# Scores and products in halves between the quarters of the solo steps, eleven chunks paired, and ScalarE in source order for two more units

## The chip, the cores and the metric

The kernel runs on one core of a Trainium2 chip, as one program. The metric is its time on the device in microseconds. Beside it stands the span, from the first to the last instruction of one profiled execution. Engines are named as in the profile: PE (TensorE's matmuls) and PEld (its weight loads), DVE (VectorE), ACT (ScalarE), POOL (GpSimd) and SP (SyncE, which issues all DMAs here).

## The reference

Attention over chunks of 32 rows with a local context and 8 memory rows, and then, for each of four batches, a mixer: a low-rank product over the sequence (U, V) and a feed-forward layer of 512 to 2048 to 512. All in float32, and U, V and the weights come as float64.

```python
for c in range(nc):                       # 768 / 32 = 24 chunks, 8 heads, D = 64
    k_full = np.concatenate([mem_k, k[:, :, l_start:r_end]], axis=2)   # 16 left, 8 right
    v_full = np.concatenate([mem_v, v[:, :, l_start:r_end]], axis=2)
    scores = scale * np.matmul(q_c, k_full.transpose(0, 1, 3, 2))
    a = np.exp(scores - np.max(scores, axis=-1, keepdims=True))
    a = a / (np.sum(a, axis=-1, keepdims=True) + 1e-09)
    out[:, :, c_start:c_end] = np.matmul(a, v_full)
...
h = xt @ U @ V                            # rank 32, over the sequence
u = x + h.transpose(0, 2, 1)
return u + np.maximum(u @ w_ch1, 0.0) @ w_ch2
```

## The kernel before, in words

**The feed-forward part.** The 2048 hidden columns are cut into 16 chunks f of 128. A batch has 768 rows in two blocks of 384. For a block and a chunk, `w1_step` runs 12 matmuls into a bank of ps_h (L943): every factor is split into a high and a low part, and three of the four products are formed. ScalarE then writes relu's high part hh (L949), VectorE the low part hl (L950). `w2_step`, always of the unit before, runs 9 matmuls into three accumulators of 128 x 512 (L986 six, L991 three). One `w1_step` and the `w2_step` of its predecessor are called a unit here.

**Batch 0 is special** (`both_blocks`). The weights arrive as float64 and are decoded while it runs, so that for the first SPLIT = 12 chunks both blocks are computed in turn (units 0 to 23; block 0 one chunk ahead, LEAD = 1). The second block's three accumulators are the three banks of ps_a, which the attention otherwise uses. When they are given up (L957 adds them to x), the remaining four chunks run solo: block 0 in units 24 to 27, and then block 1 in units 28 to 31, in the order 15, 14, 12, 13. For chunks 12 and 13 block 1 fetches the low part of w1 (w1l) back from DRAM (`fetch_w1l`, L398). During the last eleven units the attention of batch 1 is computed: its generator is advanced by steps, of which PACE counts how many are taken by the end of each unit from BEGINL = 21 on. They are taken together: up to unit 24 behind `w2_step`, later between `w1_step` and `w2_step`. In later batches the same steps are spread evenly.

**Decoding.** `stream` takes a chunk through ScalarE (L185, the exponent words scaled: the begin), five operations of VectorE (L196, L200, L210, L215, L222), ScalarE's cast of the high part (`upper`, L333) and VectorE's subtraction for the low part (`lower`, L337). Chunks 0 and 1 go w1 and w2 by themselves, later ones both at once, six steps each. Its working buffers are tiles called dec while the front runs, and the two homes of v, vb, afterwards. A chunk's begin stands in the source in the middle of the decoding of the one before. Every unit takes RATE = 3 steps, every fourth one more.

**The attention** of a batch works in pairs T = 0, 1, 2 of 128-row tiles. `k_part` and `q_part` transpose half a pair's keys or queries on PE (L476), and ScalarE copies them out of PSUM (L499 to L507, L519). `s_turn` runs the scores of a pair, 128 matmuls of 64 x 32 by 64 (L535) into two banks; `s_weights` takes maximum, difference and exponential (L557, L558 on VectorE, L561 on ScalarE), `s_sums` the sums (L566). `t_part` transposes one bank of weights (L582, copied by L585). `av_part` runs the products with v, again 128 small matmuls into two banks (L597), which VectorE scales into x (L606). `load_v` brings v with ten or eleven DMAs a pair. At the end `collect` (L617, L623) forms U's part, `gs` and `g4` (L826 to L835) follow, and six matmuls L846 with L848 add V's part to x.

**Order.** PE runs in the source's order through batch 0 (`manual`, FRONT), SyncE in the whole kernel. VectorE and ScalarE follow the source during the head of batch 0 (HEAD, to L1083), that is, the whole attention of batch 0 up to "joined"; then VectorE in a manual schedule of its own (`paced`) until unit 24. All else is ordered by a scheduler that goes by its own estimate of times and may set instructions of a free engine ahead of earlier ones of the source. The head also runs V's and U's decoding, `spread_v` (L247, L252, L253), `turn_x` (L872) and the joins (L881 to L886, L896 to L918) that make the first two blocks' inputs. LOADS is the order of the head's DMAs on SyncE: t is q and k of a pair, v and w the v of a pair and the raw weights of a chunk.

PSUM has eight banks: three of ps_a, two of ps_h, three of ps_o (the accumulators of block 0).

```python
for n, (blk, f, where, begins, ends) in enumerate(units):
    ...
    hid_ = w1_step(0, blk, f, w1l)
    ...
    if n > 2 * SPLIT:
        next(first, None)
        for _ in range(pieces[n]):
            next(gen[0], None)
    if prev is not None:
        ...
        w2_step(0, *prev)
    if n <= 2 * SPLIT:
        for _ in range(pieces[n]):
            next(gen[0], None)
```

Of the kernel before, what the change touches and what calls it, by code (L numbers as in the profile page):

```python
# [22 lines left out]
HEAD = {ET.DVE, ET.Activation}  # L23
# [3 lines left out]
LOADS = 't0 mk t1 t2 uv mv v0 mm v1 v2 w0 w1 w2'  # L27
# [3 lines left out]
HIGH = 400  # L31
LEAD = 1
SPLIT = 12
# [4 lines left out]
BEGINL = 21  # L38
NLOAD = 1
NSOLO = 2  # L40
PACE = [1, 2, 3, 9, 13, 23, 27, 30, 34, 35, 36]
# [3 lines left out]
def chunk_attn_then_mixer_kernel(  # L45
# [355 lines left out]
    def attention(b, xs):  # L401
# [123 lines left out]
        def s_turn(T):  # L525

            qt = [qts.pop((T, h)) for h in range(2)]
            banks = [att_ps() for _ in range(2)]
            psv = [ps.rearrange("n (t k g w) -> n t k g w", t=2, k=2, g=2) for ps in banks]
            for t in range(2):  # L530
                for p in range(NPR):
                    for i in range(NI):
                        for s in range(2):
                            rows = slice(D * s, D * s + D)
                            nc.tensor.matmul(  # L535
                                out=psv[s][CK * i:CK * i + CK, t, p % 2, p // 2, :],
                                lhsT=qt[p // 2][rows, p % 2, NI * t + i, :],
                                rhs=kall[rows, NB * (T % 2) + NI * t + i, p, :], start=True, stop=True,
                            )
            return banks, psv  # L540
# [31 lines left out]

        def s_part(T):
            s_weights(T, *s_turn(T))
            s_sums(T)
# [11 lines left out]
        def av_part(T):  # L587

# [3 lines left out]
            for t in range(2):  # L592
                for j in range(4):
                    for i in range(NI):
                        for g in range(2):
# [5 lines left out]
                            )  # L601
            rs = rss.pop(T)
            for t in range(2):
# [7 lines left out]
                xs[(b, 2 * T + t)] = x  # L611

# [125 lines left out]
        else:  # L738
# [36 lines left out]
            if b == 1:  # L775
                load_both(2)
                yield
                s_part(0)
                yield
# [7 lines left out]
                yield from turns(2)  # L787
                yield from turn_p(0)
                s_part(1)
                yield  # L790
                av_part(0)
                yield
                yield from load_v(2)
                yield from turn_p(1)
                s_part(2)
                yield
                yield from turn_p(2)
                av_part(1)
                yield
# [14 lines left out]
            av_part(NP - 1)  # L814
            yield
# [119 lines left out]
    def w1_step(b, blk, f, w1l):  # L935
# [6 lines left out]
        for m, (w, u, c) in enumerate(parts):  # L942
            nc.tensor.matmul(  # L943
                out=ph[:, :TOK], lhsT=w[:, c, :], rhs=u[c], start=(m == 0), stop=(m + 1 == len(parts)),
            )
        hh = hid.tile([P, TOK], F32R, name="hh")
# [16 lines left out]
    def w2_step(b, blk, f, where, begins, ends, hh, hl):  # L963
# [19 lines left out]
        for tt in range(TB):  # L983
            sl = slice(tt * P, (tt + 1) * P)
            for m, (h, w) in enumerate(passes[:2]):
                nc.tensor.matmul(  # L986
                    out=acc[tt], lhsT=h[:, sl], rhs=w, start=(begins and m == 0), stop=False,
                )
        for tt in range(TB):
# [10 lines left out]
    def both_blocks(pieces, following):  # L1000
# [11 lines left out]
        prev = None  # L1012
        paced = ExitStack()
        paced.enter_context(tc.manual_schedule(engines={ET.DVE}))
        for n, (blk, f, where, begins, ends) in enumerate(units):
            while done[0] < min(2 * NF, 2 * f + 2):
                advance(1)
                more_w()
            if n == 2 * SPLIT:
# [9 lines left out]
            hid_ = w1_step(0, blk, f, w1l)  # L1029
# [6 lines left out]
            if n > 2 * SPLIT:  # L1036
                next(first, None)
                for _ in range(pieces[n]):
                    next(gen[0], None)
            if prev is not None:  # L1040
# [3 lines left out]
                w2_step(0, *prev)  # L1044
            if n <= 2 * SPLIT:
                for _ in range(pieces[n]):
                    next(gen[0], None)
            prev = (blk, f, where, begins, ends) + hid_
        following(lambda: w2_step(0, *prev))
# [22 lines left out]
    manual.enter_context(tc.manual_schedule(engines=FRONT))  # L1072
    head = ExitStack()
# [9 lines left out]
    head.close()  # L1083
# [4 lines left out]
    for b in range(B):  # L1088
# [3 lines left out]
        for n in range(2 * NF):  # L1092
            if b == 0:
                want = PACE[n - BEGINL] if n >= BEGINL else 0
            else:
                want = min(NPIECE, -(-NPIECE * (n + 1) // (2 * NF - 2)))
# [3 lines left out]
        def following_pair(last):  # L1100
            with tc.high_priority(offset=HIGH):
                for _ in range(TB):
                    next(gen[0])
            last()
# [9 lines left out]
        if b == 0:  # L1114
            both_blocks(pcs, following_pair)
# [37 lines left out]
```

## Time and profile before

| | us |
|---|---|
| median of 3 runs | 723.65 (723.29 to 727.45) |
| the profiled execution | 724.77 |
| its span, first to last instruction | 723.0 |
| PE busy in the span | 673.6 |
| VectorE busy | 310.5 |
| ScalarE busy | 187.8 |
| mean granted clock of TensorE | 0.969 |

The times in the lines below are counted from the span's start. In a timeline line stand the start, the time that it took (of several, from the first's start to the last's end), engine and line, the operation, output and inputs, the shapes, how many; and in brackets how long the engine was idle before it and what ended that wait. In the table of waits stand the total, how many, and the longest. "Issue" is time in which an engine waited for nothing that the profile shows. PEclk is the share of full speed at which TensorE's clock was granted. SPq is SyncE's queue of DMAs.

### The profile page before, as it was taken

The page shows a single profiled execution, that of the slowest core. Times are in us where ns is not written, and L with a number is a line of the kernel's source. Part 1 is how long each engine was busy: PE and PEld are TensorE (multiplying, and loading weights), DVE is VectorE, ACT ScalarE, POOL GpSimd, SP SyncE. Part 2 cuts the span into 40 slices and gives each one's busy share as a digit, 9 for nine tenths or more (in the row PEclk, how much of TensorE's full clock was granted, in tenths as well). Part 3 has the DMA queues.
Part 4 walks back from the last instruction along what each step waited for, and adds up shares of the span by engine and source line. Part 5 has one row for each costly group of instructions (what it writes and reads, how often), then busy time and mean ns, then how long its engine had stood idle before and what let it go on. Part 6 is the DMA issues. An engine that isn't in the chain of part 4 may idle for free.

```text
span 723.0 us, 14688 instructions
## 1 busy us (share of the span) xinstructions
PE 673.6 (93%) x6280; PEld 586.6 (81%) x6284; DVE 310.5 (43%) x584; ACT 187.8 (26%) x470; POOL 22.0 (3%) x47
## 2 busy tenths in 40 slices
PE   7756999998786999999999998999999999999997
PEld 5534889987675789998888997898888999899896
DVE  6838889999644352225322230144342321112112
ACT  4423343343531122322211123133121211111110
POOL 2000000013200000000000000000000000000000
PEclk9868999999998899999999998999999999999999
DMA  8693445532642087312411076422411132214211
GB/s 233 134 344 101 138 146 168 191 94 87 160 119 82 1 232 176 117 44 85 116 48 56 30 210 157 131 70 74 125 46 45 44 102 73 61 42 131 63 55 44
DMA packets 103512, 79.07 MB, mean 109 GB/s; under 512 B 49464, under 2 KB 83384, under 8 KB 103448
## 3 DMA queue, kind: packets, MB, share of 16 engines
q1 hardware_dynamic: 103448, 78.14, 37.4%
q8 instruction: 49, 0.80, 0.5%
q14 instruction: 15, 0.12, 0.1%
HBM read 66.45 MB, written 10.49 MB: 106 GB/s over the span
## 4 chain that ended last, share of the span: by engine, by line
PE 82%; SPq 7%; DVE 5%; DMA 3%; issue 2%; ACT 1%; POOL 0%; ACTq 0%; DVEq 0%
PE ps_h L943 36%; PE acc L986 21%; PE acc L991 10%; SPq L458 3%; PE ps_a L597 2%; PE ps_a L476 2%; PE ps_a L535 2%; PE ps_a L986 2%; SPq L440 1%; PE ps_a L582 1%; PE ps_a L991 1%; DMA rw<-in_moe_w_ch_dram 1%; PE ps_a L928 1%; DVE x L957 1%; DMA w1l<-w1ld 1%
## 5 line engine op out<-in xcount | busy, mean ns | idle before, releaser
L950 DVE SCALAR_TENSOR_TENSOR hl<-ps_h,hh 128x384 fp32r<-128x384 f32 x127 | 70.5, 555 | 294.8 <-ACT hh L949 294.7
L943 PE MATMUL ps_h<-uh,w1h 128*128 128x384 f32 x508 | 171.5, 339 | 4.5 <-ACT w1h L333 3.7
L943 PE MATMUL ps_h<-ul,w1h 128*128 128x384 f32 x508 | 173.1, 342 | 0.1
L949 ACT ACTIVATE hh<-ps_h 128x384 fp32r<-128x384 f32 x127 | 62.6, 493 | 402.1 <-PE ps_h L943 402.1
L986 PE MATMUL acc<-w,hh 128*128 128x512 f32 x600 | 162.9, 405 | 0.0
L986 PEld LDWEIGHTS acc<-w,hh 128*128 128x128 f32 x600 | 110.8, 191 | 22.8 <-issue 3.4
L943 PE MATMUL ps_h<-uh,w1l 128*128 128x384 f32 x508 | 111.5, 339 | 3.1 <-DMA w1l<-w1ld 2.6
L943 PEld LDWEIGHTS ps_h<-uh,w1h 128*128 128x128 f32 x508 | 95.7, 189 | 10.4 <-ACT w1h L333 4.0
L943 PEld LDWEIGHTS ps_h<-ul,w1h 128*128 128x128 f32 x508 | 95.8, 189 | 5.7 <-DVE ul L931 0.4
L943 PEld LDWEIGHTS ps_h<-uh,w1l 128*128 128x128 f32 x508 | 90.7, 190 | 4.2 <-DMA w1l<-w1ld 2.9
L991 PE MATMUL acc<-w,hl 128*128 128x512 f32 x300 | 86.1, 392 | 0.0
L991 PEld LDWEIGHTS acc<-w,hl 128*128 128x128 f32 x300 | 56.5, 188 | 12.9
L848 DVE TENSOR_TENSOR x<-ps_a,x 128x512 f32<-128x512 f32 x24 | 16.1, 688 | 38.7 <-PE ps_a L846 38.7
L535 PE MATMUL ps_a<-kall,qt 64*32 64x64 f32 x1344 | 22.0, 225 | 3.6 <-issue 2.8
L986 PE MATMUL acc<-w2last,hh 128*128 128x512 f32 x90 | 25.1, 416 | 0.0
L535 PEld LDWEIGHTS ps_a<-kall,qt 64*32 64x32 f32 x1344 | 18.0, 105 | 7.8 <-issue 6.1
L597 PE MATMUL ps_a<-vb,pT 64*32 64x64 f32 x1152 | 15.5, 236 | 9.2 <-issue 6.1
L561 ACT ACTIVATE pt<-pt 128x512 f32<-128x512 f32 x24 | 15.0, 634 | 31.2 <-DVE pt L558 31.2
L597 PEld LDWEIGHTS ps_a<-vb,pT 64*32 64x32 f32 x1152 | 13.5, 110 | 11.6 <-issue 10.2
L606 DVE TENSOR_TENSOR x<-ps_a,rs 128x256 f32<-128x256 f32 x44 | 15.7, 413 | 13.6 <-PE ps_a L597 12.0
L986 PEld LDWEIGHTS acc<-w2last,hh 128*128 128x128 f32 x90 | 17.1, 197 | 4.2 <-issue 1.0
L499 ACT COPY kall<-ps_a 128x256 f32<-128x256 f32 x40 | 17.3, 441 | 10.5 <-PE ps_a L476 10.5
(188 smaller groups left out, 646.1 us busy)
## 6 DMA issues: line engine op xcount, KB each, us to landing
w1l<-w1ld SPq DMA_DIRECT2D x98, 256.0 KB
rw<-in_moe_w_ch_dram SPq DMA_DIRECT2D x14, 512.0 KB
qraw<-in_q_dram SPq DMA_DIRECT2D x24, 256.0 KB
out_dram<-x SPq DMA_DIRECT2D x24, 256.0 KB
vb<-in_v_dram SPq DMA_DIRECT2D x56, 98.0 KB
raw<-in_moe_w_ch_dram SPq DMA_DIRECT2D x20, 256.0 KB
kraw<-in_k_dram SPq DMA_DIRECT2D x16, 256.0 KB
rw<-in_moe_w_ch_dram SPq DMA_DIRECT2D x16, 256.0 KB
```

What stands on the lines that cost most here:

```text
L458: nc.sync.dma_start(out=vt[r0:r0 + NW - NM, n0:n1, D * j:D * j + D], in_=bass.AP(rows.tensor, rows.offset, [[step, count], [CK * step, n1 ...
L499: copy(out=kt[:, p, :, :, m:m + w], in_=psv[:, q_])
L535: nc.tensor.matmul(out=psv[s][CK * i:CK * i + CK, t, p % 2, p // 2, :], lhsT=qt[p // 2][rows, p % 2, NI * t + i, :], rhs=kall[rows, NB * ( ...
L561: nc.scalar.activation(out=pt, in_=pt, func=AF.Exp, scale=scale)
L597: nc.tensor.matmul(out=psv[g][CK * i:CK * i + CK, t, j], lhsT=pt[j % 2][rows, 2 * t + j // 2, CK * i:CK * i + CK], rhs=vt[rows, NI * t + i ...
L606: nc.vector.tensor_tensor(out=x[:, 4 * D * g:4 * D * g + 4 * D].rearrange("n (j d) -> n j d", d=D), in0=psv[g][:, t], in1=rs[:, t, g].rear ...
L848: nc.vector.tensor_tensor(out=x, in0=hp, in1=x, op=ALU.add)
L943: nc.tensor.matmul(out=ph[:, :TOK], lhsT=w[:, c, :], rhs=u[c], start=(m == 0), stop=(m + 1 == len(parts)),)
L949: nc.scalar.activation(out=hh, in_=ph[:, :TOK], func=AF.Relu)
L950: nc.vector.scalar_tensor_tensor(out=hl, in0=ph[:, :TOK], scalar=0.0, in1=hh.bitcast(F32), op0=ALU.max, op1=ALU.subtract,)
L986: nc.tensor.matmul(out=acc[tt], lhsT=h[:, sl], rhs=w, start=(begins and m == 0), stop=False,)
L991: nc.tensor.matmul(out=acc[tt], lhsT=hl[:, sl], rhs=w2h[f], start=False, stop=ends is not None)
```

## The change

The change has five parts, in the diff below.

1. `s_turn` and `av_part` become generators of two halves (`s_halves`, `av_halves`: t = 0 and t = 1, 64 matmuls each), and batch 1's attention yields between them. Both banks are held over both halves; weights, sums and scaling follow the second. The keys of pair 2 are turned behind the scores of pair 0 rather than behind v's loads. The steps to "joined" grow from 36 to 42.
2. `w1_step` and `w2_step` call a function `between` in their middle (after 6 of 12 matmuls, and after the first 6 of 9), and `both_blocks` calls it behind each of them too. PLACE says for units 20 to 31 how many steps are taken by each of the four places. The three first h steps of the attention's end are set into the middle of the last `w2_step`.
3. SPLIT is 11: eleven chunks are paired (units 0 to 21), five run solo (units 22 to 26, and 27 to 31 in the order 15, 14, 11, 12, 13). Block 1 fetches w1l of three chunks instead of two, and VectorE's manual schedule ends at unit 22.
4. ScalarE's source order (HEAD) ends at unit 2 instead of at "joined". VectorE's (PACED) is one schedule from the start to unit 22 instead of two.
5. In LOADS the raw weights of chunk 0 come ahead of v of pair 2.

```diff
-HEAD = {ET.DVE, ET.Activation}
+PACED = {ET.DVE}
+HEAD = {ET.Activation}
-LOADS = 't0 mk t1 t2 uv mv v0 mm v1 v2 w0 w1 w2'
+LOADS = 't0 mk t1 t2 uv mv v0 mm v1 w0 v2 w1 w2'
-SPLIT = 12
+SPLIT = 11
-BEGINL = 21
-PACE = [1, 2, 3, 9, 13, 23, 27, 30, 34, 35, 36]
+PLACE = {
+    20: [0, 0, 0, 1], 21: [0, 0, 0, 2], 22: [0, 0, 0, 3], 23: [4, 5, 6, 7], 24: [8, 9, 10, 12], 25: [13, 14, 15, 16],
+    26: [17, 18, 20, 22], 27: [23, 24, 25, 26], 28: [27, 28, 30, 31], 29: [32, 33, 34, 35], 30: [36, 36, 37, 38],
+    31: [39, 40, 40, 41],
+}
...
         def s_turn(T):
+            *_, last = s_halves(T)
+            return last
+
+        def s_halves(T):
...
-            return banks, psv
+                yield banks, psv
...
+        def s_parts(T):
+            for t, made in enumerate(s_halves(T)):
+                if t:
+                    s_weights(T, *made)
+                    s_sums(T)
+                yield
...
         def av_part(T):
+            for _ in av_halves(T):
+                pass
+
+        def av_halves(T):
...
+                if t == 0:
+                    yield
...
             if b == 1:
                 load_both(2)
                 yield
-                s_part(0)
-                yield
+                yield from s_parts(0)
+                turning = turns(2)
+                for _ in range(2):
+                    next(turning)
+                    yield
+                yield from turn_p(0)
                 while done[0] < 2 * NF:
...
-                yield from turns(2)
-                yield from turn_p(0)
-                s_part(1)
-                yield
-                av_part(0)
-                yield
+                yield from turning
+                yield from s_parts(1)
+                yield from av_halves(0)
                 yield from load_v(2)
                 yield from turn_p(1)
-                s_part(2)
-                yield
+                yield from s_parts(2)
+                yield from av_halves(1)
                 yield from turn_p(2)
-                av_part(1)
-                yield
+                yield from av_halves(2)
...
-    def w1_step(b, blk, f, w1l):
+    def w1_step(b, blk, f, w1l, between=lambda: None):
...
+            if m + 1 == len(parts) // 2:
+                between()
...
-    def w2_step(b, blk, f, where, begins, ends, hh, hl):
+    def w2_step(b, blk, f, where, begins, ends, hh, hl, between=lambda: None):
...
+        between()
         for tt in range(TB):
             sl = slice(tt * P, (tt + 1) * P)
             nc.tensor.matmul(out=acc[tt], lhsT=hl[:, sl], rhs=w2h[f], start=False, stop=ends is not None)
...
-        prev = None
-        paced = ExitStack()
-        paced.enter_context(tc.manual_schedule(engines={ET.DVE}))
+        prev, taken = None, [0]
...
+            if n == 2:
+                head.close()
             if n == 2 * SPLIT:
                 paced.close()
...
-            hid_ = w1_step(0, blk, f, w1l)
+            placed = iter(PLACE.get(n, ()))
+
+            def between():
+                upto = next(placed, 0)
+                while taken[0] < upto:
+                    next(gen[0])
+                    taken[0] += 1
+
+            hid_ = w1_step(0, blk, f, w1l, between)
...
             if n > 2 * SPLIT:
                 next(first, None)
-                for _ in range(pieces[n]):
-                    next(gen[0], None)
+            between()
...
-                w2_step(0, *prev)
-            if n <= 2 * SPLIT:
-                for _ in range(pieces[n]):
-                    next(gen[0], None)
+                w2_step(0, *prev, between)
+            between()
...
-        following(lambda: w2_step(0, *prev))
+        following(lambda between: w2_step(0, *prev, between))
...
+    paced = ExitStack()
+    paced.enter_context(tc.manual_schedule(engines=PACED))
     head = ExitStack()
     head.enter_context(tc.manual_schedule(engines=HEAD))
...
-    head.close()
...
         def following_pair(last):
-            with tc.high_priority(offset=HIGH):
-                for _ in range(TB):
-                    next(gen[0])
-            last()
+            next(gen[0])
+
+            def mixed():
+                with tc.high_priority(offset=HIGH):
+                    for _ in range(TB):
+                        next(gen[0])
+
+            last(mixed)
             make_uT(1, 0)
```

More of the change, by code (lines that the diff above doesn't have):

```diff
@@ L777, in attention @@
                 yield
-                s_part(0)
-                yield
+                yield from s_parts(0)
+                turning = turns(2)
+                for _ in range(2):
+                    next(turning)
+                    yield
+                yield from turn_p(0)
                 while done[0] < 2 * NF:
@@ L813, in attention @@
                     yield from turn_p(T)
-            av_part(NP - 1)
-            yield
+                av_part(NP - 1)
+                yield
         if b > 0:
@@ L998, in get_w1l, with both_blocks @@
             w1ls[f] = fetch_w1l(f)
-    def both_blocks(pieces, following):
+    def both_blocks(following):
         units = []
@@ L1092, in chunk_attn_then_mixer_kernel @@
         for n in range(2 * NF):
[L1093 to L1096, printed above, removed]
+            want = min(NPIECE, -(-NPIECE * (n + 1) // (2 * NF - 2)))
             pcs.append(want - given)
@@ L1114, in chunk_attn_then_mixer_kernel @@
         if b == 0:
-            both_blocks(pcs, following_pair)
+            both_blocks(following_pair)
             continue
```

## The prediction

> **What bounds the kernel now.** I read the page first (what is busy), then the windows (which stage is not), then the timeline of each engine in the two stages that are not, then the table of who waited for whom there, and the chain of waits for the places between.
>
> ```profile
> span 723.0 us, 14688 instructions
> PE 673.6 (93%) x6280; PEld 586.6 (81%) x6284; DVE 310.5 (43%) x584; ACT 187.8 (26%) x470; POOL 22.0 (3%) x47
> q8 instruction: 49, 0.80, 0.5%
> ```
>
> The page says that TensorE is the bound on average, with some 50 us in which it has no matmul. The windows (stretch; length, then busy time of PE, PEld, DVE, ACT, POOL with counts; granted clock; DMA share; GB/s) say where those lie:
>
> ```profile
> 36.00:54.00 18.00, 8.97 (x132) 6.41 (x124) 5.50 (x13) 4.29 (x11) 0.00 (x0) 0.69 0.99 339
> 78.38:163.16 84.78, 84.29 (x422) 75.79 (x420) 76.91 (x117) 34.98 (x76) 2.91 (x4) 1.00 0.44 143
> 163.16:203.78 40.62, 32.78 (x292) 27.59 (x291) 28.80 (x49) 19.41 (x63) 9.36 (x11) 0.96 0.52 139
> 203.78:255.82 52.04, 42.10 (x804) 34.55 (x803) 24.32 (x51) 9.79 (x18) 2.01 (x6) 0.90 0.18 55
> 255.82:723.00 467.18, 460.44 (x3799) 409.45 (x3799) 128.36 (x252) 92.24 (x227) 2.68 (x8) 0.99 0.33 91
> ```
>
> The last row is batches 1 to 3 behind the pair of blocks: PE is busy there to 99%, and the change touches none of it. The paired stretch (second row) is PE's as well, with VectorE at 91%. What can be won lies in the head (first row: 9 us without a matmul, clock at 0.69) and between 163.16, where unit 22 begins, and 255.82, where batch 1 begins: 92.66 us of which PE is busy 74.88.
>
> **The head: ScalarE's order and the place of w0.** ScalarE, VectorE, PE and SyncE's queue:
>
> ```profile
> 46.22 0.97 ACT L185 ACTIVATE vb<-rw 128x512 f32<-128x512 f32 x2 [14.98 <-DMA raw<-in_moe_w_ch_dram]
> 48.41 0.66 ACT L185 ACTIVATE vb<-rw 128x512 f32<-128x512 f32 x1 [0.80 <-DMA rw<-in_moe_w_ch_dram]
> 48.97 0.35 ACT L252 CAST v<-ps_a 96x256 fp32r<-96x256 f32 x1
> ```
>
> ```profile
> 38.27 0.41 DVE L606 TENSOR_TENSOR x<-ps_h,rs 128x256 f32<-128x256 f32 x1
> 55.66 1.42 DVE L606 TENSOR_TENSOR x<-ps_a,rs 128x256 f32<-128x256 f32 x4 [1.97 <-PE ps_a L597]
> 68.67 0.69 DVE L222 TENSOR_TENSOR dec<-dec 128x512 f32<-128x512 f32 x1
> ```
>
> ```profile
> 37.19 0.86 PE L247 MATMUL ps_a<-dec,rep 32*96 32x256 f32 x2
> 39.88 1.50 PE L872 MATMUL ps_h<-ident,x 128*128 128x128 f32 x12
> 50.16 2.93 PE L872 MATMUL acc<-ident,x 128*128 128x128 f32 x12 [8.79 <-DVE v L253]
> 70.12 1.65 PE L943 MATMUL ps_h<-uh,w1h 128*128 128x384 f32 x4 [3.73 <-ACT w1h L333]
> ```
>
> ```profile
> 30.00 1.92 SPq L458 DMA_DIRECT2D vbe<-in_v_dram  x4
> 36.46 0.44 SPq L293 DMA_DIRECT2D rw<-in_moe_w_ch_dram  x1
> ```
>
> ScalarE stands still for 14.98 us until 46.22 for raw weights, and what it then writes is vb, not dec. In the code vb is the home of decoded words only after the front: these are the words of chunk 1's w2 and of chunk 2, begun in the source inside unit 0. The scheduler has put them ahead of the L252 casts of V, which come earlier in the source and need no weight at all. Behind L252 waits VectorE's L253, behind that the bank that the second half of turn_x (L872) wants, and behind that all of the head. With ScalarE in source order until unit 2, both of these begins (in steps of the weight stream taken before and after unit 0's first matmuls) stand behind V's casts, so the 14.98 us wait has no one left behind it.
>
> What is late next: V's matmuls (L247) are done at 38.05, so L252 can run then. VectorE ends the four L606 of pair 1 at 38.68 and does the three L253, as long as L606 has it at most (0.41 each, overlapping: some 1.1 us), to 39.8. PE has the first 12 L872 until 41.4, so the second 12 follow without a wait and at 1.50 us rather than 2.93: to 42.9. Two warm-up matmuls, say 0.6, and pair 2's product, 1.7 (a part of as many matmuls takes 1.48 in a row further down): L606 at 45.2 instead of 55.66, which is 10.5 us earlier. From there to chunk 1's last decoding step (68.67) VectorE is the chain, 13 us nearly without a gap, and PE's unit 1 waits for just that (70.12, 3.73 us behind ScalarE's w1h). VectorE now keeps one source order from the head into the pair, which moves U's part (L835, L886) ahead of the decoding but adds no work; I take 0.5 us more from gaps closed. **Head: 11 us.** From below 9, if PE stays at the cold clock (1.4 us on L872 and as much on the product); from above 12.5.
>
> The move of w0 serves the same point: unit 0's words are begun right behind L252, at about 39, and VectorE wants them at 39.8. Its three DMAs go out at 30.0 instead of 36.46, ten issues earlier. The slowest weight DMA of the head took 6.71 us:
>
> ```profile
> 41.61 6.71 DMA rw<-in_moe_w_ch_dram
> 196.54 3.07 DMA vb<-in_v_dram
> ```
>
> so w0 has landed by 31.4 + 6.7 = 38.1. Without the move it would be up to 44.6, and the decoding would end after 45.2: worth 0 to 3 us, and inside the 11. The last v2 DMAs go out some 1.5 us later, at 37.9 instead of 36.4; a v DMA is 3.07 us on the way in the second row, so v2 is there at 41 and is wanted at 43.5. Chunks 1 to 4 keep their place. The paired units then run as before, 11 us earlier: the same steps of the decoding stand between the same units.
>
> **The solo stage, from unit 22.** A unit has a pitch of 4.19 us (its 12 L943 begin that far apart on the chain):
>
> ```profile
> 159.13 2.10 PE ps_h L943 x12
> 163.32 2.10 PE ps_h L943 x12
> ```
>
> Ten units from 163.16 are in both kernels, whatever their chunk; so are all pieces of batch 1's attention. Eleven chunks paired instead of twelve only make the pieces start at unit 23 rather than 24, and cost one more 256 KB fetch of w1l, on a DMA system at 0.52. What changes is what PE waits for. Who waited for whom, 150 to 262 (total, times, longest):
>
> ```profile
> PE ps_a L597 <- issue: 6.1, 3, 3.1
> PE ps_a L535 <- issue: 2.8, 1, 2.8
> PE ps_a L476 <- DVE x L957: 2.3, 1, 2.3
> PE ps_a L597 <- DVE pt L558: 1.9, 1, 1.9
> PE ps_a L476 <- issue: 1.6, 3, 1.0
> ```
>
> With four smaller ones (1.2, 0.8, 0.6, 0.4) they make 17.7 us. The clock adds 40.62 x 0.04 + 52.04 x 0.10 = 6.8. So 24.5 us are to be had; what stays of them, term by term:
>
> (a) "Issue" inside a run of small matmuls is the instruction stream.
>
> ```profile
> 191.63 0.44 PE L535 MATMUL ps_a<-kall,qt 64*32 64x64 f32 x10 [2.83 <-issue]
> 192.00 2.86 PE L986 MATMUL acc<-w,hh 128*128 128x512 f32 x6
> 197.73 1.04 PE L476 MATMUL ps_a<-ident,kn 128*128 128x128 f32 x8
> 206.21 1.48 PE L535 MATMUL ps_a<-kall,qt 64*32 64x64 f32 x128
> 229.57 0.64 PE L597 MATMUL ps_a<-vb,pT 64*32 64x64 f32 x21 [3.12 <-issue]
> 251.50 1.55 PE L986 MATMUL acc<-w,hh 128*128 128x512 f32 x6
> ```
>
> The page has 49 packets of 16 KB on the instruction queue and 12,564 PE instructions: 256 to a packet. A scores or product part is 128 matmuls and 128 weight loads, one packet's worth, gone in 1.48 us. Twice a part stopped some 20 matmuls before its end, for 2.83 and 3.12 us, and twice more for 1.8 and 1.1; the part at 206.21 did not stop. After the change a half with a half unit of big matmuls around it takes about 1.8 us, so a packet lasts some 3.5 us instead of 1.5. That is near the length of the stops, and the six packets that end inside a part still do so. Bounds: 0 (all hidden) and 6 x 2.1 = 13; I take 4.5, nearer the rows that stopped, since scores 2 and products 1 still stand close. The Trainium skill ("Runtime: NRT & Kernel Launch", Instruction fetch mechanics) says that crossing such a boundary is mostly hidden, because the next page is fetched while the present one runs. By that rule this term is 0 and the time 698.5; the stops of 2.83 and 3.12 us speak against it here.
>
> (b) L957 frees the three ps_a banks of the pair. Now it stands a whole unit ahead of the first transposes but for half a step: unit 21's w2 ends at 167.3, L957 takes 0.7 a bank (its row stands below), VectorE may be in the middle of a decoding step of 1.2, and the first transposes come 1.05 us on: 0.7 us, about the middle of 0 and 0.9, instead of 2.3.
>
> (c) VectorE. The solo chunks are wanted one unit earlier (chunk 13 at unit 24, 14 at 25, 15 at 26), and units now go by faster.
>
> ```profile
> 163.47 1.10 DVE L337 TENSOR_TENSOR w<-vb,w 128x512 fp32r<-128x512 f32 x1
> 187.51 0.68 DVE L337 TENSOR_TENSOR w1l<-vb,w1h 128x512 fp32r<-128x512 f32 x1
> L957 DVE TENSOR_TENSOR x<-ps_a,x 128x512 f32<-128x512 f32 x3 | 1.9, 682 | 0.0
> L557 DVE TENSOR_REDUCE mx<-ps_a 128x8 f32<-128x512 f32 x2 | 1.3, 686 | 0.0
> L558 DVE TENSOR_TENSOR pt<-ps_a,mx 128x512 f32<-128x512 f32 x2 | 1.3, 681 | 0.0
> ```
>
> From 163.47 to 188.2 it is all but continuously at the decoding. In unit 25 it must also have emptied both score banks (L557, L558: 2.6) and done two more L848 (of L957's shape, 0.68 each) before k's transposes of pair 2 find a bank, while the last w1l may wait: 188.2 + 4.0 - 0.7 = 191.5. PE would be there at 163.16 + 4.2 (unit 22) + 0.7 + 6.5 + 6.5 (units 23, 24 with four transposing pieces of 0.52, two in the 1.04 of the row at 197.73, and L846) + 5.7 (half of unit 25 and more) = 186.8. Late by 4.7; VectorE's few gaps may be used, and I take 4. Bounds 0 and 8.
>
> (d) In units 27 to 30 two products' halves follow scores by half a unit, 1.05 us, and want a bank that VectorE frees 1.4 us behind: about 1 us twice, 2. (e) The gather of pair 2 now stands in unit 31's last quarter, so that the copy of its sum on ScalarE lies bare before L829: 1, an estimate. (f) batch 1's first wait on uh stays, 0.8. (g) The slow clock follows the gaps (192.00: 2.86 us for six matmuls, 1.55 at 251.50); with shorter gaps I keep 2 of the 6.8.
>
> What stays: 4.5 + 0.7 + 4 + 2 + 1 + 0.8 + 2 = 15. **Solo: 24.5 - 15 = 9.5 us.** SyncE's queue: the new fetch of chunk 13's w1l waits for a buffer until unit 28's first matmuls, and holds behind it only v2's loads, which wait for pair 0's product in the same unit anyway, and are wanted three units (some 18 us) later. Nothing in batches 2 and 3 changes but where a yield stands: 0.
>
> **Sum.** 11 + 9.5 = 20.5 us off the span of 723.0, 702.5. The profiled execution took 724.77, 1.8 above its span; the median of three runs is 723.65, 0.65 above it. So 723.65 - 20.5, which I round to 703.
>
> **Rivals.** First, that the quarters hide all: terms (a), (c) and (d) vanish and the solo stage gives 20: 723.65 - 31 = 692.7. For it: pieces a quarter apart give every bank a half unit; against: VectorE's 24.7 us without a gap. Second, VectorE or the instruction stream becomes the bound and eats the solo gain (term (c) at 8, (a) at 10): 712.6. For it: VectorE at 91% before the stage begins. Third, the change doesn't do in the head what it says: source order makes ScalarE wait for w0 and later weights in front of its own casts, and the 15 us come back: 723.65 - 9.5 = 714.2. Against: all weights of chunks 0 to 2 had landed by 48.4, and in source order they are wanted later than that or w0 early. Fourth, slower: every one of the 12 halves runs the instruction stream dry, as three of six parts do now. At 3 us each that is 36 instead of 4.5, and the time 703 + 31.5 = 734.5; it is slower than before from 2.2 us a half on (20.5 + 4.5 over 12 is 2.1). Against: 49 packets in all, of which only some eight fall into the stage.
>
> **Chances.** The forecast 0.58 (its own range 697 to 709), all hidden 0.18, solo gain eaten 0.13, head not won 0.07, slower 0.04. From 692 to 714 leaves out the last case and the edges of the first and third. What a measurement of this kernel can tell from no change is about 1%, 7 us: the first three cases and most of the fourth lie under 716.4, so faster 0.92, same 0.04, slower 0.04.
>
> **What would show it.** In the changed profile: no L185 on vb ahead of L252, L252 near 38 to 39; L872's second half right behind the first; unit 1's L943 near 59; batch 1's first L943 between 233 and 237. Right for the solo stage: an "issue" total of 3 to 7 us, L957 under 1 us, and a wait on VectorE's scores or decoding in units 25 to 26. Wrong: L252 still behind a weight (head), PE's waits from unit 22 on over 18 us in sum, or another instruction of the weight stream as the new end of the 15 us gap.

## The result and the profile after

The changed kernel took 698.82 us (median of 4 runs, 698.16 to 701.36) beside 723.47 for the kernel before in the same session: a ratio of 0.967, with a 95% interval from 0.960 to 0.974. That is 24.7 us less; the prediction said 20.5 less, to 703. The profiled execution took 701.36, its span is 699.6. Line numbers are 4 to 24 higher than before: V's casts L252 are now L256, turn_x L872 is L894, the products L597 are L616 and their evacuation L606 is L627, the scores L535 are L543, the transposes L476 and L582 are L480 and L597, L943 is L965, L957 is L981.

Lines of the page of the kernel after, to be laid beside those of before:

```profile
span 699.6 us, 14688 instructions
PE 666.4 (95%) x6284; PEld 577.2 (83%) x6284; DVE 311.2 (44%) x584; ACT 187.6 (27%) x470; POOL 23.4 (3%) x47
```

The windows of the kernel after (stretch; length, busy time of PE, PEld, DVE, ACT, POOL; granted clock; DMA share; GB/s), cut at the same places of the program: head, pair, solo stage in two parts and as a whole, the rest.

```profile
36.00:54.00 18.00, 15.19 (x283) 10.11 (x269) 10.44 (x26) 5.42 (x15) 0.00 (x0) 0.90 0.90 261
62.82:155.44 92.62, 92.13 (x456) 83.27 (x457) 84.30 (x129) 39.11 (x86) 3.05 (x4) 0.98 0.47 150
155.44:187.63 32.19, 30.05 (x287) 25.57 (x285) 30.60 (x51) 18.40 (x60) 10.77 (x11) 1.00 0.44 125
187.63:233.38 45.75, 42.12 (x811) 32.37 (x809) 22.33 (x47) 11.40 (x22) 2.02 (x6) 1.00 0.34 85
155.44:233.38 77.94, 72.17 (x1096) 57.94 (x1094) 52.93 (x98) 29.80 (x82) 12.79 (x17) 1.00 0.38 102
233.38:699.60 466.22, 458.17 (x3799) 406.86 (x3799) 129.48 (x254) 92.20 (x227) 2.65 (x8) 1.00 0.33 92
```

Of the 23.4 us of span, 7.7 were won before unit 22 (163.16 to 155.44), 14.7 in the solo stage (92.66 to 77.94) and 1.0 behind it. The solo stage splits further: TensorE's busy time fell from 74.88 (32.78 + 42.10) to 72.17 for the same matmuls, while the clock granted over the stage rose from 0.93 to 1.00, and the rest of the stretch, in which it has no matmul, fell from 17.8 to 5.8. So 12.0 us are waits and 2.7 go with the clock. In the head, ScalarE, TensorE and VectorE of the kernel after show the order that was asked for:

```profile
39.58 0.37 ACT L256 CAST v<-ps_a 96x256 fp32r<-96x256 f32 x1 [7.57 <-PE ps_a L251]
40.38 0.44 ACT L189 ACTIVATE dec<-rw 128x256 f32<-128x256 f32 x1
58.57 0.66 ACT L189 ACTIVATE vb<-rw 128x512 f32<-128x512 f32 x1
```

```profile
38.63 0.21 PE L616 MATMUL ps_h<-vb,pt 64*32 64x64 f32 x1 [1.70 <-issue]
43.23 1.50 PE L894 MATMUL ps_h<-ident,x 128*128 128x128 f32 x12
44.56 1.50 PE L894 MATMUL acc<-ident,x 128*128 128x128 f32 x12
62.82 0.69 PE L965 MATMUL ps_h<-uh,w1h 128*128 128x384 f32 x1 [6.59 <-ACT w1h L337]
```

```profile
47.96 1.42 DVE L627 TENSOR_TENSOR x<-ps_a,rs 128x256 f32<-128x256 f32 x4 [3.25 <-PE ps_a L616]
```

V's casts come at 39.58, with no raw weight for vb ahead of them; the first of those follows at 58.57. The second half of turn_x stands right behind the first and no longer 8.79 us later. But pair 1's product stops for 1.70 us at 38.63 on "issue", which the kernel before did not do, and unit 1 begins at 62.82, 7.3 us earlier than 70.12 and not 11.

TensorE's waits from 150 to 240 in the kernel after (total, times, longest). They make 6.2 us; the kernel before had 17.7 from 150 to 262. The last, 0.4, stands behind the solo stage:

```profile
PE ps_a L616 <- DMA vb<-in_v_dram: 1.2, 1, 1.2
PE ps_a L616 <- issue: 1.0, 1, 1.0
PE ps_a L480 <- DVE x L981: 0.9, 1, 0.9
PE ps_a L851 <- ACT gs L848: 0.7, 1, 0.7
PE ps_h L965 <- ACT uh L952: 0.7, 1, 0.7
PE ps_a L597 <- ACT pt L569: 0.6, 1, 0.6
PE ps_a L480 <- issue: 0.6, 1, 0.6
PE ps_a L868 <- DVE ul L953: 0.4, 1, 0.4
```

### The profile page after: what moved, and what is told of

It reads as the page before. It is cut to its first block, busy times and chain, and to the rows that moved or that the text cites. A ratio compares the mean times of both kernels' runs of the same rounds, so it can differ in the third digit from the quotient of the medians.

```text
span 699.6 us, 14688 instructions
## 1 busy us (share of the span) xinstructions
PE 666.4 (95%) x6284; PEld 577.2 (83%) x6284; DVE 311.2 (44%) x584; ACT 187.6 (27%) x470; POOL 23.4 (3%) x47
## 4 chain that ended last, share of the span: by engine, by line
PE 81%; DVE 9%; DMA 4%; SPq 3%; issue 2%; ACT 1%; POOL 0%; ACTq 0%; DVEq 0%; POOLq 0%
PE ps_h L965 35%; PE acc L1010 21%; PE acc L1016 10%; PE ps_a L616 2%; PE ps_a L543 2%; PE ps_a L480 1%; PE ps_a L1010 1%; PE acc L639 1%; DVE vb L219 1%; DVE vb L204 1%; PE ps_a L597 1%; DMA w1l<-w1ld 1%; SPq L462 1%; PE ps_a L950 1%; DMA rw<-in_moe_w_ch_dram 1%
## 5 line engine op out<-in xcount | busy, mean ns | idle before, releaser
L965 PE MATMUL ps_h<-uh,w1h 128*128 128x384 f32 x508 | 172.9, 342 | 7.3 <-ACT w1h L337 6.6
L965 PE MATMUL ps_h<-ul,w1h 128*128 128x384 f32 x508 | 173.1, 342 | 0.1
L965 PE MATMUL ps_h<-uh,w1l 128*128 128x384 f32 x508 | 110.8, 338 | 3.7 <-DMA w1l<-w1ld 3.2
L965 PEld LDWEIGHTS ps_h<-uh,w1h 128*128 128x128 f32 x508 | 95.7, 189 | 13.4 <-ACT w1h L337 6.9
L965 PEld LDWEIGHTS ps_h<-ul,w1h 128*128 128x128 f32 x508 | 95.9, 189 | 5.4 <-DVE ul L953 0.4
L965 PEld LDWEIGHTS ps_h<-uh,w1l 128*128 128x128 f32 x508 | 90.3, 189 | 5.0 <-DMA w1l<-w1ld 3.8
L1010 PE MATMUL acc<-w2last,hh 128*128 128x512 f32 x90 | 23.7, 399 | 0.0
L543 PEld LDWEIGHTS ps_a<-kall,qt 64*32 64x32 f32 x1344 | 17.9, 105 | 5.3 <-issue 4.5
L543 PE MATMUL ps_a<-kall,qt 64*32 64x64 f32 x1344 | 21.9, 224 | 0.0
L981 DVE TENSOR_TENSOR x<-acc,x 128x512 f32<-128x512 f32 x24 | 15.4, 685 | 11.4 <-PE acc L1016 9.8
L627 DVE TENSOR_TENSOR x<-ps_a,rs 128x256 f32<-128x256 f32 x44 | 15.7, 414 | 7.8 <-PE ps_a L616 5.1
L204 DVE SCALAR_TENSOR_TENSOR vb<-vb 128x1024 int32<-128x1024 int32 (+1 forms) x15 | 18.1, 1208 | 0.3
```

The lines of the kernel that those rows point to most:

```text
L204: nc.vector.scalar_tensor_tensor(out=ti, in0=yi, scalar=-2 ** 31, in1=ti, op0=ALU.bitwise_and, op1=ALU.bitwise_or,)
L543: nc.tensor.matmul(out=psv[s][CK * i:CK * i + CK, t, p % 2, p // 2, :], lhsT=qt[p // 2][rows, p % 2, NI * t + i, :], rhs=kall[rows, NB * ( ...
L627: nc.vector.tensor_tensor(out=x[:, 4 * D * g:4 * D * g + 4 * D].rearrange("n (j d) -> n j d", d=D), in0=psv[g][:, t], in1=rs[:, t, g].rear ...
L965: nc.tensor.matmul(out=ph[:, :TOK], lhsT=w[:, c, :], rhs=u[c], start=(m == 0), stop=(m + 1 == len(parts)),)
L981: nc.vector.tensor_tensor(out=x, in0=bank, in1=x, op=ALU.add)
L1010: nc.tensor.matmul(out=acc[tt], lhsT=h[:, sl], rhs=w, start=(begins and m == 0), stop=False,)
```

## Experiments

The theory ahead of the experiments: two gains that do not touch each other, the head's from ScalarE's order and the solo stage's from halves, which keep the instruction stream ahead of TensorE, and from quarters, which give banks and VectorE room. The rivals: w0's early load carries the head; the halves do nothing; the solo stage gains only because the head lets it begin earlier.

**The two halves of the change, each alone, and w0.** Run one is the kernel before with the head's parts:

```
-HEAD = {ET.DVE, ET.Activation}
-LOADS = 't0 mk t1 t2 uv mv v0 mm v1 v2 w0 w1 w2'
+PACED = {ET.DVE}
+HEAD = {ET.Activation}
+LOADS = 't0 mk t1 t2 uv mv v0 mm v1 w0 v2 w1 w2'
...
+            if n == 2:
+                head.close()
...
```

> Kernel before with parts 4 and 5 alone: ScalarE in source order for two more units, w0 ahead of v2. Theory (two separate gains, head and solo stage): V's cast near 39.6 us, unit 1 near 62.8, unit 22 near 155.4, and the solo stage as long as before, 92 to 93 us: time 715 to 716.5. Rival (the early start of the pair only makes the solo stage wait longer for the decoding or for v, so a part is given back): solo stage 95 us or more, time 718 or more.

Run two is the kernel after with the old LOADS, and with HEAD closed at "joined" again. Of part 4 one thing stays in it: VectorE's manual schedule is one from the start to unit 22.

> Kernel after with parts 4 and 5 undone: halves, quarters and 11 paired chunks alone. Theory (two separate gains): V's cast near 49 us as before, unit 22 near 163, solo stage 77 to 79 us, time 706 to 707.5. Rival (the solo stage gained more than forecast because the decoding has a head start from the head): solo stage 81 us or more, time above 710.

Run three is the kernel after with the old LOADS alone:

> Kernel after with the old order of loads (w0 behind v2), ScalarE's order kept. Theory (the order of ScalarE carries the head, the move of w0 is worth 0 to 3 us): time 699 to 702, V's cast still near 39.6. Rival (w0 is what V's chain waits for): unit 1 some 6 us later, time near 705.

The head alone: 716.08 (8 runs), ratio 0.991 (0.988 to 0.994), 7.0 us less than the 723.08 beside it. The solo part alone: 708.92, ratio 0.982 (0.977 to 0.987), 14.2 less. Without the early w0, with all else of the change: 698.39, ratio 0.967 (0.962 to 0.973). Solo stages of the three, in that order, each from the windows of its own kernel:

```profile
153.21:249.18 95.97, 78.79 (x1096) 66.06 (x1094) 53.51 (x100) 29.50 (x82) 11.00 (x17) 0.88 0.32 88
```

```profile
163.67:242.94 79.27, 72.27 (x1095) 57.90 (x1093) 52.86 (x97) 29.55 (x81) 13.37 (x18) 1.00 0.37 100
```

```profile
152.45:231.34 78.89, 72.28 (x1096) 57.93 (x1094) 53.02 (x98) 29.76 (x82) 13.44 (x18) 1.00 0.37 100
```

The move of w0 is worth nothing that shows: without it V's casts come at 38.08 and unit 1 at 59.65. The order of ScalarE carries the head. With the head alone unit 1 began at 59.88, 10.2 us earlier than before; yet the median fell by only 7.0. The profiled execution doesn't say where the rest went. Its span is 712.8 beside 723.0, the full 10.2 less: the solo stage took 3.3 us more than before (95.97 beside 92.66), and the stretch behind it, which the change does not touch, 3.6 less (463.62 beside 467.18). In the solo stage the time without a matmul is about that of before (17.2 beside 17.8); TensorE is busy for 78.79 us instead of 74.88, at a granted clock of 0.88 instead of 0.93. So the theory of run one has the time right and the stage wrong, and the rival has the stage's 95 us or more right and its mechanism wrong: the waits did not grow in sum, the clock was lower. Why it was lower is not settled by one profile. Without the head the solo stage is as short as with it, so its gain does not need the earlier start. The two gains alone make 21.2 of 24.7 us.

**Are the halves worth it?** Two runs take each scores and product part whole, first at the place of its first half, then of its second:

```
-    ... 25: [13, 14, 15, 16],
+    ... 25: [14, 14, 15, 16],
...
-    27: [23, 24, 25, 26], 28: [27, 28, 30, 31], 29: [32, 33, 34, 35],
+    27: [23, 24, 26, 26], 28: [28, 28, 30, 31], 29: [32, 34, 34, 36],
...
-    31: [39, 40, 40, 41],
+    31: [40, 40, 40, 41],
```

> Kernel after with the same places, but each scores and product part whole in the place of one of its halves, 128 matmuls in a row. Theory (halves hide the instruction stream: the page of 256 lasts 1.5 us instead of 5): issue stops of 1.8 to 3.1 us in two or three of the six parts come back, 4 to 7 us, time 703 to 706. Rival (the quarter places for banks and VectorE do the work, halves are worth nothing): time 698 to 700.

```
-    ... 25: [13, 14, 15, 16],
+    ... 25: [12, 14, 15, 16],
...
-    27: [23, 24, 25, 26], 28: [27, 28, 30, 31], 29: [32, 33, 34, 35],
+    27: [23, 24, 24, 26], 28: [26, 28, 30, 31], 29: [32, 32, 34, 34],
...
-    31: [39, 40, 40, 41],
+    31: [38, 40, 40, 41],
```

> Kernel after with whole parts, each in the place of its second half (in the earlier run of whole parts: of its first). Theory (the quarter places win, halves as such nothing): solo stage 76 to 77.5 us, no wait of a product for a score bank, time within 1.5 us of the kernel after. Rival (whole parts run the instruction stream dry in some executions, which one profile need not show): time 3 us or more above the kernel after, as the median of the earlier run of whole parts was (702.5).

And the kernel after once more beside the second of them:

> The kernel after, unchanged, beside the three that follow. Theory (the 1.04 us wait in pair 1's product is the score bank that VectorE frees, not a transfer or an instruction page): it comes back with the same length, and ends when the first of the two subtractions that follow the scores ends. Rival (instruction pages): its length changes from one execution to the next as the stop in the head did (0 to 1.7 us). Time 698 to 700 by both.

The first took 702.54 (698.60 to 705.30), the second 700.94 (697.65 to 704.56), the kernel after 701.42 (696.64 to 704.37). With so wide a spread the three cannot be told apart. The first kernel's largest wait, on VectorE, in its timeline, then its solo stage and that of the second kernel, which are as short as with halves:

```profile
179.74 0.63 PE L480 MATMUL ps_a<-ident,kn 128*128 128x128 f32 x4 [2.62 <-DVE pt L566]
```

```profile
153.89:230.39 76.50, 69.64 (x1096) 58.14 (x1094) 52.88 (x98) 30.08 (x82) 12.86 (x17) 1.00 0.39 104
```

```profile
156.38:234.08 77.70, 71.51 (x1096) 59.68 (x1094) 52.87 (x98) 29.73 (x82) 13.55 (x18) 0.98 0.38 102
```

No stop of 2 to 3 us came back in a whole part. What "issue" is left inside one is 1.73 us in the first kernel, behind the first two matmuls of a product that follows scores, and 0.90 and 0.51 in the second, in the middle of products. My theory that the halves keep the instruction stream fed falls: they are worth nothing that these runs show.

**The wait in the products: a transfer, the stream, or a bank?** In the kernel after, the first halves of two products begin with two matmuls and then wait; one wait is put down to v's transfer and one to "issue". VectorE and TensorE there:

```profile
195.47 1.28 DVE L565 TENSOR_REDUCE mx<-ps_a 128x8 f32<-128x512 f32 x2
196.66 1.28 DVE L566 TENSOR_TENSOR pt<-ps_a,mx 128x512 f32<-128x512 f32 x2
197.55 0.83 PE L616 MATMUL ps_a<-vb,pT 64*32 64x64 f32 x62 [1.19 <-DMA vb<-in_v_dram]
...
209.96 0.30 PE L616 MATMUL ps_a<-vb,pT 64*32 64x64 f32 x2
210.52 1.28 DVE L566 TENSOR_TENSOR pt<-ps_a,mx 128x512 f32<-128x512 f32 x2
211.30 0.83 PE L616 MATMUL ps_a<-vb,pT 64*32 64x64 f32 x62 [1.04 <-issue]
```

Both times TensorE goes on 0.1 to 0.2 us behind the end of the first of the two L566 (0.68 us each, so about 197.3 and 211.2), that is when the first of the two score banks has been read for the last time. In the repeat the waits were 1.17 and 1.05 us, both put down to "issue", with the same neighbours: the length does not vary as that of the stop in the head did. One run sets these products a quarter later:

```
-    28: [27, 28, 30, 31], 29: [32, 33, 34, 35], 30: [36, 36, 37, 38],
+    28: [26, 27, 30, 31], 29: [32, 33, 34, 34], 30: [35, 36, 37, 38],
```

> Kernel after with the halves of pair 0's and pair 1's products set one quarter later (two quarters instead of one behind the scores). Theory (1.19 and 1.04 us are waits for a score bank, 1.4 us of VectorE behind the scores): both waits go, solo stage 75.5 to 76.5, time 2 us lower than the kernel after. Rival (1.19 is v's transfer, 1.04 the instruction stream): the transfer's wait shrinks by at most a quarter's 1 us, the other stays; time 0 to 1 us lower.

```profile
196.02 0.27 PE L616 MATMUL ps_a<-vb,pT 64*32 64x64 f32 x2 [0.25 <-PE ps_a L868]
196.52 0.83 PE L616 MATMUL ps_a<-vb,pT 64*32 64x64 f32 x62 [0.23 <-issue]
208.73 1.12 PE L616 MATMUL ps_a<-vb,pT 64*32 64x64 f32 x64
```

```profile
153.73:230.05 76.32, 72.10 (x1095) 57.84 (x1093) 52.84 (x98) 29.62 (x82) 13.49 (x18) 1.00 0.38 104
```

Both waits are gone but for 0.23 us, and the stage is 1.7 us shorter than the 78.04 of the kernel after beside it. The bank theory holds: the length stays from one execution to the next, the end goes with L566, and a quarter's delay takes the wait away. The name "DMA vb" in the table of waits was wrong. The time, 701.18 (696.94 to 705.22), does not show 1.7 us within its spread.

**Instruction pages.** The kernel before with 16 more matmuls in the first warm-up:

```
+PAD = 16
...
+        if warm[0] == START:
+            for _ in range(PAD):
+                nc.tensor.matmul(out=ps[0:32, 0:32], lhsT=busy[0:64, 0:32], rhs=busy[0:64, 0:32], ...)
```

> Kernel before with 16 more tiny matmuls (32 columns, output not used) in the first warm-up of the head, while PE waits for data anyway. Theory (stops inside small parts are page ends of the instruction stream, 256 instructions apart): each stop moves 16 matmuls towards the front of its part, so about 93 matmuls instead of 109 or 105 stand before the stop and some 37 behind it; lengths may change since the page is asked for earlier; time 715 to 727. Rival (the stops belong to a bank, a semaphore or the place in the part): they stay where they are, about 20 matmuls before the end.

The kernel before in products 1 and 2 (its stop in the scores is the row at 191.63 above, x10 behind 2.83 us):

```profile
225.06 1.39 PE L597 MATMUL ps_a<-vb,pT 64*32 64x64 f32 x109 [1.16 <-DVE x L848]
229.57 0.64 PE L597 MATMUL ps_a<-vb,pT 64*32 64x64 f32 x21 [3.12 <-issue]
231.33 1.82 PE L597 MATMUL ps_a<-vb,pT 64*32 64x64 f32 x105 [1.12 <-issue]
234.96 0.64 PE L597 MATMUL ps_a<-vb,pT 64*32 64x64 f32 x21 [1.81 <-issue]
```

The padded kernel's stops in the scores and in product 2, and its solo stage:

```profile
188.81 0.43 PE L539 MATMUL ps_a<-kall,qt 64*32 64x64 f32 x26 [1.38 <-issue]
227.87 0.63 PE L601 MATMUL ps_a<-vb,pT 64*32 64x64 f32 x37 [1.27 <-issue]
```

```profile
161.95:247.10 85.15, 72.44 (x1095) 60.41 (x1093) 53.37 (x99) 29.21 (x81) 12.06 (x18) 0.98 0.36 100
```

26 matmuls behind the stop instead of 10, and 37 instead of 21: both stops moved by exactly the 16 matmuls that were added in the head, some 180 and 220 us earlier. So their place is a count of instructions: they are ends of pages, of 256 instructions by the count of the packets. The stop of 3.12 us is gone and these two are shorter. The one of 1.12 us did not move and is as long (1.14): in both kernels it stands behind the first two matmuls of product 2, as the bank waits of the kernel after do, so it is more likely a bank. And 16 matmuls whose output nobody uses made the kernel faster by 6.9 us (4 to 11 by the interval): 715.81 beside 722.70, ratio 0.990 (0.984 to 0.995).

**Where the pieces stand.** Two runs take back the rest of the solo part. One has 12 chunks paired:

```
-SPLIT = 11
+SPLIT = 12
-    20: [0, 0, 0, 1], 21: [0, 0, 0, 2], 22: [0, 0, 0, 3], 23: [4, 5, 6, 7], 24: [8, 9, 10, 12], 25: [13, 14, 15, 16],
-    26: [17, 18, 20, 22], ...
+    20: [0, 0, 0, 1], 21: [0, 0, 0, 2], 22: [0, 0, 0, 3], 23: [0, 0, 0, 3], 24: [0, 0, 0, 3], 25: [6, 9, 11, 12],
+    26: [13, 14, 16, 18], ...
```

> Kernel after with 12 chunks paired instead of 11; the first transposes then start at unit 25, and 12 pieces of attention are pressed into units 25 to 27. Theory (the eleventh chunk only moves the start of the pieces by one unit; what it is worth is the room it gives VectorE): waits on VectorE of 2 to 4 us in units 25 to 27 in place of 1.25, time 701 to 704. Rival (the room is not used): same time as the kernel after within 1 us, solo stage 77 to 79.

The other puts the pieces of a unit at one place. Scores and products are then whole, but for product 1, whose halves fall into units 29 and 30:

```
+    20: [0, 1], 21: [0, 2], 22: [0, 3], 23: [0, 7], 24: [0, 12], 25: [0, 16],
+    26: [0, 22], 27: [0, 26], 28: [0, 31], 29: [0, 35], 30: [0, 38], 31: [0, 41],
```

> Kernel after with all pieces of a unit at one place, between its w1 and its w2, instead of in four quarters; parts are then whole. Theory (the quarters carry the solo stage's gain): waits of TensorE of 10 to 14 us from unit 22 to batch 1 instead of 5.1, solo stage 83 to 88, time 706 to 711. Rival (the early start with 11 chunks and the new order of the pieces carry it): waits of 5 to 7, solo stage 77 to 80, time 700 to 703.

Twelve chunks: 700.22, ratio 0.970 (0.966 to 0.974). One place a unit: 702.20, ratio 0.973 (0.968 to 0.977). The solo stage of each, and the largest wait of the second:

```profile
153.26:231.84 78.58, 72.42 (x1095) 58.03 (x1093) 53.04 (x98) 29.71 (x82) 11.43 (x17) 1.00 0.36 98
```

```profile
152.78:232.66 79.88, 72.79 (x1096) 59.96 (x1094) 52.25 (x98) 29.70 (x82) 14.15 (x18) 0.98 0.37 99
```

```profile
PE ps_a L615 <- DVE pt L565: 2.0, 1, 2.0
```

Both rivals held. By these profiles the eleventh chunk is worth 0.6 us of the stage and quarters with halves together 1.9, of 14.7. The wait of 2.0 us is a product right behind the scores of the next pair, the same bank wait as above, here under its own name.

**The page in the head.** Pair 1's product stopped there in eight of the nine profiled executions so far that hold the new order, for 0.72 to 3.68 us. The new order is not needed for it: the padded kernel before stopped there for 2.04. Two runs shift the pages in the kernel with the later products, by 40 and by 16 matmuls:

> Kernel after with pair 0's and pair 1's products a quarter later and 40 tiny matmuls (output not used) in the head's first warm-up. Theory (the stop in pair 1's product in the head, 0 to 3.7 us in seven executions, is a page whose request goes out at about 29 us and then waits 6 to 7 us; 80 instructions earlier it goes out at about 27): no stop or one under 1 us in that product, unit 1 near 60, time 697 to 699. Rival (the request waits for the same transfers whenever it is sent): a stop of 1 to 4 us stays, 40 matmuls nearer to the product's start, time 700 to 702.

> As the run with 40 tiny matmuls, with 16. Theory (page ends): stop in pair 1's product in the head 16 matmuls nearer to its start than in the kernel after, shorter than 1.5 us since the request goes out some 1.5 us earlier; time 697 to 700. Rival (the request waits for the same transfers): 1 to 4 us, time 700 to 702.

With 40, pair 1's product does not stop, and unit 1 begins at 59.15; with 16 it stops for longer than ever:

```profile
59.15 1.33 PE L969 MATMUL ps_h<-uh,w1h 128*128 128x384 f32 x3 [6.59 <-ACT w1h L341]
```

```profile
151.78:228.05 76.27, 72.09 (x1096) 57.85 (x1094) 52.77 (x98) 29.59 (x82) 12.86 (x17) 1.00 0.38 104
```

```profile
40.30 0.26 PE L620 MATMUL ps_h<-vb,pt 64*32 64x64 f32 x1 [4.90 <-issue]
```

Behind it 26 matmuls of the product are left, in the kernel after 10: this stop too moves with the 16 that were added, so it is a page's end. The transfers of that second kernel, from 30.1 to 37.5 and from 37.5 to 40.3 (q1 is the queue of the kernel's own DMAs, q8 with its 49 packets TensorE's instructions, q14 another queue of instructions):

```profile
DMA packets 2642, 1.54 MB, mean 208 GB/s; under 512 B 2001, under 2 KB 2513, under 8 KB 2641
q1 hardware_dynamic: 2641, 1.53, 86.1%
q14 instruction: 1, 0.01, 0.3%
```

```profile
q8 instruction: 1, 0.02, 3.1%
```

No packet of TensorE's instructions moves for 7.4 us while 2,641 of q1 and one of q14 do; then one does, and TensorE goes on. The 40 brought 696.42 us (694.57 to 700.87), ratio 0.965 (0.960 to 0.969), the lowest median of the study; the 16 brought 700.29, ratio 0.969. The expectation for the 16 failed: it named a stop under 1.5 us. That for the 40 was right in its result, not in its reason. Counted back 256 instructions from the place of the stop, TensorE passed the end of the page before at about 29.6, no earlier than in the others (29.2 to 30.8), and the next packet came 1.1 us later, with q1 at 92%, instead of some 4.6 to 7.5. Why a packet is held up once and not another time stays open. Whether this version is faster than the kernel after is likely from its profile (no stop in the head, a stage of 76.27) and not settled in time, since the intervals overlap.

## Why the prediction was right, and where it was not

**The sum was nearer than its terms.** Of the span 7.7 us were won ahead of unit 22 and not 11, 14.7 in the solo stage and not 9.5, and 1.0 behind it and not 0. That the time came out 4.2 us from the forecast is in part luck: the errors have opposite signs.

**Head, 11 us predicted, 7.3 found at unit 1.** The mechanism held step by step: casts, turn_x's second half, no wait for a weight. Its size held where pair 1's product did not stop. L627 of pair 2 was forecast at 45.2 and unit 1 near 59; run three and the run with 40 more matmuls, neither with a stop in pair 1's product, show VectorE there at

```profile
44.81 1.42 DVE L627 TENSOR_TENSOR x<-ps_a,rs 128x256 f32<-128x256 f32 x4 [1.64 <-PE ps_a L616]
```

```profile
44.29 1.42 DVE L631 TENSOR_TENSOR x<-ps_a,rs 128x256 f32<-128x256 f32 x4 [1.64 <-PE ps_a L620]
```

and unit 1 at 59.65 and 59.15. In the profile of the kernel after, L627 came at 47.96: 1.70 us went at the page's end, and the four collects behind it then took 3.58 us instead of 1.96 before (0.86 us apart instead of 0.43; the granted clock was 0.50 from 39.8 to 43.1). Whether the stop brings the low clock is not shown: in the repeat a stop of 2.18 was followed by four collects in 1.96 us. The step that failed is that the prediction looked for page ends in the solo stage alone, in term (a), and had none in the head.

**w0, "0 to 3 us, inside the 11".** Nothing that shows: unit 1 is no later without the move.

**Solo stage, 9.5 us predicted, 14.7 found.** The two sums differ by term like this. (a) Stops in small parts, 4.5 kept: in this profile none; 0.6 and 1.2 in runs three and two. (The stop of 1.1 us that the prediction counted with the others is the one that did not move with the 16 matmuls.) (b) L957, now L981, 0.7: 0.9. (c) VectorE, 4: 1.25, as a wait for ScalarE's exponentials of pair 0's scores (0.65) and one of 0.6 before the keys of pair 2 are turned. The profile puts that one down to "issue"; at the same place the run with whole parts waits 2.62 us and names VectorE, so it is probably the wait that was forecast, shorter. (d) Products behind scores, 2: 1.19 + 1.04 = 2.2; the run with the later quarter shows what they are. (e) 1: 0.71. (f) 0.8: 0.67, and 0.44 more behind it. So (b), (d), (e) and (f) were right to 0.3 each, and (a) and (c) too large by 4.5 and 2.75: 13 us of waits were kept in the sum and 6.2 are there. (g) The clock went to 1.00, so nothing of it stayed. But the 6.8 us that I had put to be had from it were taken on the whole stretch, waits included, and a low clock costs only while TensorE works: in the kernel before it was busy for 6.50 of the 10.20 us from 228.8 to 239.0, all at 0.50. The busy time fell by 2.7, not by the 4.8 of the sum; busy time alone, with the two rows' clocks, would still give 5.5 in place of 6.8, so this explains only part of the gap, and the rest stays open. The clock took back 2.1 of what (a) and (c) had given.

**What carried the solo stage.** By the runs neither halves, nor quarters (with halves, 1.9), nor the eleventh chunk (0.6). What all the short variants share, and the kernel before has not, is the order of the pieces and their spread over the units: before, products 1 and 2 stand behind one another from 225.06 to 235.6, with 1.16, 3.12, 1.12 and 1.81 us of waits among them, 7.2 in all; after, a unit of large matmuls stands between any two products. That this is the cause is argued by elimination and from those rows; no run took the order alone. Part of the 14.7 is where the page ends fell in the kernel before: with 16 matmuls added its stage took 85.15 us instead of 92.66, and beside that the change gains 7.2. In the same session the medians were 715.81 with the 16 and 701.42 for the kernel after. The ten kernels with the new solo part lie between 76.27 and 79.88, wherever their pages end.

**The instruction stream as such.** That the stops which moved are ends of pages is now shown (16 matmuls in, 16 matmuls moved). The Trainium skill ("Runtime: NRT & Kernel Launch", Instruction fetch mechanics) has such a crossing mostly hidden. In the solo stage after the change the traces agree, with 0 to 1.4 us in all; in the head they do not, with 0.72 to 4.90 us for one crossing in nine of the eleven profiled executions with the new head. The 698.5 that the prediction worked out for term (a) at 0 is the measured time by coincidence: (a) did vanish, but the head, (c) and the clock were off as well.

**Signs named ahead.** L252 free of weights, turn_x's halves together, batch 1's first L943 between 233 and 237 (233.38), L957 under 1 us: as said. Unit 1 near 59: 62.82 here. "Issue" of 3 to 7 us in the solo stage: 1.6, of which 1.04 is the bank. A wait on VectorE in units 25 to 26: only the 0.6 of (c), not under that name. That batch 1 began inside 233 to 237 is luck in part, by the two opposite errors.

## What to carry to other kernels

Where an in-order engine shows a long wait, look first at whom it holds up: taking ScalarE's instructions on late weights away from in front of V's casts brought unit 1 forward by 10 to 11 us in the two runs where pair 1's product did not stop. Runs of some hundred tiny matmuls can stop where pages of instructions end; the versions with large work between them lost 0 to 1.4 us to it in this stage, the kernel before 7.8. When two versions differ by a per cent for no reason, shift the page before explaining the rest. A wait that the profile puts down to a transfer or to "issue" may be a bank: look for what ends at the same moment in several executions.

## What the runs showed of the hardware that was not expected

Sixteen matmuls of 32 columns, in the head, changed the time of the kernel before by 6.9 us. The next page of TensorE's instructions can come some 7.5 us after TensorE has passed the end of one, while other transfers keep the DMA engines 86% busy; at nearly the same moment in another kernel, with them 92% busy, it came after 1.1. In the kernel after, the 128x512 matmuls behind the stop of 1.70 us came 0.86 us apart instead of 0.43, at a granted clock of 0.50, so that unit 1 lost 3.2 us against run three and not 1.7.
